# Top-k attention with a token and channel mixer: six of nine probability tiles masked on GpSimd before the exponential and transposed by DMA

## The chip, the cores and the metric

The kernel runs on one core of a Trainium2 chip, in one launch. The metric is the time of that core on the device, in microseconds (us), lower is better; the time of a kernel is the median of its runs. One further execution was recorded by the hardware profiler; its span runs from the core's first to its last instruction.

In the text, PE is TensorE's matmul stream, PEld its weight loads, DVE is VectorE, ACT is ScalarE, POOL is GpSimd and SP is SyncE, whose queue issues the DMAs here. L385 is line 385 of the kernel.

## The reference, cut to what matters

```python
# q, k, v: (8, 8, 576, 64); top_k = 32
scores = (1 / np.sqrt(64)) * np.matmul(q, k.transpose(0, 1, 3, 2))
kth    = np.partition(scores, -32, axis=-1)[..., -32:-31]    # 32nd largest of each row
scores = np.where(scores >= kth, scores, -1e9)
attn   = np.exp(scores - scores.max(-1, keepdims=True))
attn   = attn / (attn.sum(-1, keepdims=True) + 1e-9)
x      = np.matmul(attn, v)               # heads side by side: (8, 576, 512)
h      = np.maximum(x^T @ w_tok1, 0) @ w_tok2 ;  u  = x + h^T      # 576 -> 256 -> 576
h2     = np.maximum(u @ w_ch1, 0) @ w_ch2     ;  out = u + h2      # 512 -> 1536 -> 512
```

Each row of 576 scores keeps its 32 largest; the rest must count as nothing after the exponential.

## The kernel before, in words

**Units and tiles.** The work is 32 units (`NU`), each one batch and one pair of heads. A unit has nine score tiles of 128 rows by 576 columns: tiles 0 to 7 are query block `t = i // 2` of head `i % 2`, tile 8 holds the last 64 rows of both heads. Tiles 0 to 3 form group 0, tiles 4 to 8 group 1. After every fourth unit a batch is whole and its channel mixer runs (`h2_mm`, `out_mm`), spread between the units that follow.

**One group, in order.** PE forms the scores in PSUM (`s0_mm`, `s1_mm`, `st_mm`); ACT copies them into `SS` (four buffers, one per group) or `St` (tile 8). DVE then finds the 32nd largest value of each row. `upper` (L350) takes the larger of each pair of scores 288 columns apart into `hi`; `split4` (L374, twice) pairs `hi` once more into `hh` (larger) and `hl` (smaller). `top_round` takes the eight largest of `hh` per tile (L385) and strikes them out (L388), four rounds. `low_round` takes the eight largest of `hl` and of `lo` (L398), and `combine` (L406, L413, L415, L419) merges the lists into a column of `kthall`, the threshold. `lo`, the smaller of each first pair, is made on POOL from the bits: `both_bits` (L356) adds the two scores' bit patterns and `lower_bits` (L365) subtracts that of the larger. Both L350, L374, L406 and L415 on DVE and L356, L365 on POOL read two tensors from SBUF.

**Masking and transposing.** `expo` (ACT, L456) writes `E`, the exponential of all 576 scores, less the row's maximum (`nmax`, POOL, L447). A mask `U` is above zero where a score lies below the threshold: on ACT in one step for tiles 1, 3, 5, 7, 8 (`below_act`, L492), on POOL in two for tiles 0, 2, 4, 6 (`below` into `z`, L469, then `clamp`, L477), and on DVE in the last group (`below_dve`, L485). PE transposes by matmul against the identity (`both_tr`, L498 for `E`, L501 for `U` against the identity times -2^100) and sums both in PSUM, so that masked places sink far below zero. ACT copies out through a Relu into `PT` (`p_ev`, L521, L525; the last 64 columns of up to four tiles together, `ptail_ev`, L541, L549). `o_mm` (L562) multiplies `PT` by the values, with a column of ones that gives the row sums; DVE inverts the sums (`o_den`, L574, L575) and ACT scales into `Xb` (`o_ev`, L585).

**What sets the order.** The instructions' order on each engine is laid down ahead of time by `Plan`: each step is a task with an engine, a cost, a priority (`U = 100 * u` for unit `u`, plus an offset), its predecessors and the buffers that it takes and gives back; `order` plays this forward and emits the tasks as they would start. On the chip each engine works through its list in that order and waits on semaphores. `hold` and `later` keep POOL's masks of one group behind `lower_bits` of the next. Loads and stores stand on SP's queue (`load_one` L229, `out_st` L698). The weights' casts on POOL (L742) fall into the first units.

At the end an exact second pass runs if a check on `low8` and `kthall` (L1045 to L1055) finds a row whose lists of eight were too short.

Of the kernel before, what the change touches and what calls it, by code (L numbers as in the profile page):

```python
# [12 lines left out]
RSLACK = 3.0  # L13
ACTMASK = (1, 3, 5, 7, 8)
PE_RATE = 0.85
# [90 lines left out]
def kernel(  # L106
# [54 lines left out]
    stp = pool("stp", 2)  # L161
    gp = pool("gp", 2)
    eep = pool("eep", 9)
    uup = pool("uup", 8)
# [39 lines left out]
    for t in lbufs:  # L204
        nc.gpsimd.memset(t[:, :, :, 0:1], BIG)
    kthall = const.tile([P, NU * NTILE], f32, tag="kthall")
    low8 = const.tile([P, NU * NTILE, 2], f32, tag="low8")
# [3 lines left out]
    }  # L211
    ctr = {"vb": 0, "lb": 0}

# [123 lines left out]
    def srow(st, i):  # L337
        return st["St"][:, :] if i == 2 * NT else st["SS", i // 4][:, i % 4, :]

    def halves(st, g):  # L340
        SS = st["SS", g]
        yield slice(0, 4), SS[:, :, 0:HALF], SS[:, :, HALF:S]
        if g:
            St = st["St"]
            yield 4, St[:, 0:HALF], St[:, HALF:S]
# [7 lines left out]
    def both_bits(st, g):  # L353
        x = lists["lo"]
        for at, left, right in halves(st, g):
            nc.gpsimd.tensor_tensor(  # L356
                out=x[:, at, :].bitcast(i32), in0=left.bitcast(i32), in1=right.bitcast(i32),
                op=ALU.add,
            )
        st["lo"] = x  # L360
# [92 lines left out]
    def expo(st, i):  # L453
        g, a = grp(i)
        E = eep.tile([P, S], bf16, name="E", tag="E")
        nc.scalar.activation(  # L456
            out=E[:, :], in_=srow(st, i), func=AF.Exp,
            bias=st["nmax", g][:, a : a + 1], scale=scale,
        )
        st["E", i] = E  # L460

# [4 lines left out]

    def below(st, i):
        z = gp.tile([P, S], bf16, name="z", tag="z")
        nc.gpsimd.tensor_scalar(  # L469
            out=z[:, :], in0=srow(st, i), scalar1=-1.0, scalar2=kcol(st, i),  # L470
            op0=ALU.mult, op1=ALU.add,
        )
        st["z", i] = z

    def clamp(st, i):
        U = uup.tile([P, S], bf16, name="U", tag="U")
        nc.gpsimd.tensor_scalar(  # L477
            out=U[:, :], in0=st.pop(("z", i))[:, :], scalar1=BIG, scalar2=0.0,
            op0=ALU.min, op1=ALU.max,
        )  # L480
        st["U", i] = U

    def below_dve(st, i):
# [53 lines left out]
    def ptail_ev(st, tiles):  # L537
        PT, tl = pt_tile(st), st.pop(("tpl", tiles[0]))
        if len(tiles) > 1:
            t0 = tiles[0] // 2  # L540
            nc.scalar.activation(  # L541
                out=PT[0:TAIL, :, NT, t0 * P : (t0 + 2) * P].rearrange(
                    "p h (t q) -> p t h q", t=2
                ),
                in_=tl[0:TAIL, :].rearrange("p (t h q) -> p t h q", t=2, h=2),
                func=AF.Relu,
            )
        else:
            nc.scalar.activation(  # L549
                out=PT[0:TAIL, :, NT, W:S],  # L550
                in_=tl[0:TAIL, 0:P].rearrange("p (h q) -> p h q", h=2),
                func=AF.Relu,
            )
# [141 lines left out]
    def out_st(mst, sc, b):  # L695
# [10 lines left out]
            ldq=2, ldk=2, ldv=2, vb=NVB, qkT=2, SS=4, St=2, tp=2, s0=3, O=1, mps=2,  # L706
            E=9, U=8, z=2, A=3, lb=2, nmax=3, PT=2, Xb=2, H1T=2, UT=2, H2T=1, ob=2, den=4,
        )
# [65 lines left out]
    later = []  # L774
    masks = []
    chain = {}
# [3 lines left out]
    def plan_unit(u):  # L780
# [22 lines left out]
        )  # L803
        kd, selE, keep = {}, {}, {}
        smm = []
        nms = {}
        for g in range(2):
# [32 lines left out]
            x = add("DVE", 0.30 * n + 0.15, U + 5 * g, lambda g=g: split4(st, g), deps=[x, chain.get("low")])  # L840
            nm = None
            for r in range(TOPK // 8):
                x = add("DVE", (0.21 + (0.28 if r < 3 else 0)) * n, U + 5 * g,
                        lambda g=g, r=r: top_round(st, g, r), deps=[x],
                        acq=[("A", u, g), ("nmax", u, g)] if r == 0 else [])
                if r == 0:
                    nm = add("POOL", 0.25, U - 1000, lambda g=g: neg_max(st, g), deps=[x])
                    lob = add("POOL", 0.65 * n + 0.1, U - 1000, lambda g=g: both_bits(st, g), deps=[nm, chain.get("low")])
                    lob = add("POOL", 0.65 * n, U - 1000, lambda g=g: lower_bits(st, g), deps=[lob])
                    nms[g] = chain["bits"] = lob  # L850
                    for t in later:
                        pl.after(t, lob)
                    later.clear()
                    if g == 0:
                        pl.after(vc, lob)
            x = add("DVE", 0.21 * n, U + 5 * g, lambda g=g: low_round(st, g, 1), deps=[x], acq=[("lb", u, g)])
            x = add("DVE", 0.36 * n, U + 5 * g, lambda g=g: low_round(st, g, 0), deps=[x, lob])
            chain["low"] = x
            x = add("DVE", 0.19 * n + 0.2, U + 5 * g, lambda g=g: combine(st, g, u), deps=[x])
            keep[g] = add("POOL", 0.5, U + 5, lambda g=g: keep_low8(st, g, u), deps=[x], rel=[("lb", u, g)])  # L860
            exps = []
            for i in gtiles(g):
                exps.append(
                    add("ACT", 0.66, U - 50 + i, lambda i=i: expo(st, i), deps=[nm] + exps[-1:] + evs, acq=[("E", u, i)])
                )
            kd[g] = x
            selE[g] = exps
        PTd = {}
        pte = []
        hold = {0: [], 1: later}  # L870

        def evict(dur, prio, fn, tr, key):
            e = add("ACT", dur, prio, fn, deps=[tr] + pte[:1],
                    acq=[] if pte else [("PT", u)], rel=[key])
            pte.append(e)
            return e

        tails = []
        for g in range(2):
            ms, mains = [], []  # L880
            allms = list(masks)
            masks.clear()
            if not (last and g == 1):
                hold[g].append(keep[g])
            order = sorted(gtiles(g), key=lambda i: (i not in ACTMASK, i))
            for at, i in enumerate(order):
                a, w = i - 4 * g, U + 4 * g + at
                if last and g == 1:
                    m = add("DVE", 0.45, w + 20, lambda i=i: below_dve(st, i), deps=[kd[g]] + allms[-4:], acq=[("U", u, i)])
                elif i in ACTMASK:  # L890
                    m = add("ACT", 0.66, w - 20, lambda i=i: below_act(st, i), deps=[kd[g]] + allms[-5:], acq=[("U", u, i)])
                else:
                    x = add("POOL", 0.75, w, lambda i=i: below(st, i), deps=[kd[g]] + ms[-1:], acq=[("z", u, i)])
                    m = add("POOL", 0.68, w - 0.5, lambda i=i: clamp(st, i), deps=[x], acq=[("U", u, i)], rel=[("z", u, i)])
                    hold[g].append(x)
                ms.append(m)
                masks.append(m)
                tr = add("PE", 0.58, w, lambda i=i: p_tr(st, i), deps=[m, selE[g][a]], acq=[("tp", u, i)])
                mains.append(tr)
                PTd[i] = (evict(0.52, w + 20, lambda i=i: p_ev(st, i), tr, ("tp", u, i)))  # L900
            add("POOL", 0.0, U - 1000, lambda: None, deps=ms + selE[g],
                rel=[("SS", u, g), ("A", u, g), ("nmax", u, g)] + ([("St", u)] if g else []))
            for part, tiles in enumerate([list(range(4 * g, 4 * g + 4))] + ([[2 * NT]] if g else [])):
                tr = add("PE", 0.15 * len(tiles), U + 4 * g + 5, lambda tiles=tiles: ptail_tr(st, tiles),
                         deps=mains + selE[g], acq=[("tp", u, "l", tiles[0])],
                         rel=[(r, u, i) for r in "EU" for i in tiles])
                tails.append(
                    evict(0.5 if len(tiles) > 1 else 0.17, U + 30, lambda tiles=tiles: ptail_ev(st, tiles), tr,
                          ("tp", u, "l", tiles[0]))
                )  # L910
        for t in hold[0]:
            pl.after(t, nms[1])
# [142 lines left out]
    with tc.If(flag != 0):  # L1055
        with tc.For_i(0, B, 1) as bv:
            mst = {}
            for p in range(NPAIR):
                st = {}
                for name, src in (("q", q), ("k", k), ("v", v)):  # L1060
# [7 lines left out]
                for g in range(2):  # L1068
# [13 lines left out]
                    for i in gtiles(g):  # L1082
                        expo(st, i)
                        below(st, i)
                        clamp(st, i)
                        p_tr(st, i)
                        p_ev(st, i)
# [52 lines left out]
```

## Time and profile before

| | us |
|---|---|
| three runs: median, lowest, highest | 1067.17, 1065.01, 1068.78 |
| profiled execution, its own time | 1066.77 |
| its span | 1065.0 |
| first DVE instruction of the selection (L350) starts | 15.85 |
| DVE's last threshold (L419) ends | 995.8 |

The page of the profile gives each engine's busy time, share of the span and number of instructions; then 40 slices of the span with a digit for the busy share; then the chain of work that ended last; then groups of instructions with their busy time, the mean of one in ns, and the idle time of the engine just before them with the instruction that ended it. Busy time counts overlapped instructions once, so a group's busy time can be less than its count times its mean. From the trace come three more views: waits (engine and line, what was waited for, sum, times, longest), the timeline (start, duration, engine, line), and windows (busy time of each engine in a stretch with the granted TensorE clock).

| group | count | mean ns |
|---|---|---|
| L385 DVE MAX8, 144 columns | 1152 | 291 |
| L350 DVE TENSOR_TENSOR, 1152 columns | 64 | 1522 |
| L356 and L365 POOL TENSOR_TENSOR, 1152 columns | 96 | 2632, 2630 |
| L469, L477 POOL TENSOR_SCALAR, 576 columns | 126 each | 810, 685 |
| L456, L492 ACT ACTIVATE, 576 columns | 288, 157 | 779, 790 |
| L521 ACT ACTIVATE, 512 columns | 256 | 607 |
| L498 and L501 PE MATMUL, 128 columns, into tpp | 1152 each | 232 |

### The profile page before, as it was taken

The page shows a single profiled execution, that of the slowest core. Times are in us where ns is not written, and L with a number is a line of the kernel's source. Part 1 is how long each engine was busy: PE and PEld are TensorE (multiplying, and loading weights), DVE is VectorE, ACT ScalarE, POOL GpSimd, SP SyncE. Part 2 cuts the span into 40 slices and gives each one's busy share as a digit, 9 for nine tenths or more (in the row PEclk, how much of TensorE's full clock was granted, in tenths as well). Part 3 has the DMA queues.
Part 4 walks back from the last instruction along what each step waited for, and adds up shares of the span by engine and source line. Part 5 has one row for each costly group of instructions (what it writes and reads, how often), then busy time and mean ns, then how long its engine had stood idle before and what let it go on. Part 6 is the DMA issues. An engine that isn't in the chain of part 4 may idle for free.

```text
span 1065.0 us, 23797 instructions
## 1 busy us (share of the span) xinstructions
PE 958.3 (90%) x8058; PEld 572.4 (54%) x8058; DVE 955.8 (90%) x4087; ACT 868.2 (82%) x2008; POOL 635.8 (60%) x626
## 2 busy tenths in 40 slices
PE   7778878999898999999999998999999999899895
PEld 4444545546455556555555565556555555555542
DVE  4999999998999999999999989999799979999501
ACT  5667787988989979988989799898789789898522
POOL 3686667665766576657666666667367647666300
PEclk9676798999989998999989999899989989899878
DMA  7423111012201121112120113002211021000001
GB/s 176 154 73 93 34 35 34 2 32 60 57 12 35 33 59 24 34 45 64 40 57 13 52 29 79 13 20 67 48 25 35 31 50 35 12 2 31 16 2 48
DMA packets 123572, 46.86 MB, mean 44 GB/s; under 512 B 115952, under 2 KB 116528, under 8 KB 123440
## 3 DMA queue, kind: packets, MB, share of 16 engines
q1 hardware_dynamic: 123440, 45.24, 16.4%
q8 instruction: 65, 1.06, 0.4%
q14 instruction: 67, 0.55, 0.2%
HBM read 35.78 MB, written 9.44 MB: 42 GB/s over the span
## 4 chain that ended last, share of the span: by engine, by line
DVE 39%; PE 39%; ACT 17%; issue 1%; DMA 1%; POOL 1%; SPq 0%; DVEq 0%; ACTq 0%; POOLq 0%
DVE A L385 10%; DVE hh L388 10%; PE ps L680 7%; PE s L300 7%; DVE lb L398 6%; PE O L562 5%; PE ps L650 5%; DVE hi L350 5%; ACT E L456 5%; PE tpp L498 3%; PE tpp L501 2%; DVE hh L374 2%; ACT U L492 2%; DVE hl L374 2%; ACT SS L310 2%; ACT PT L521 2%
## 5 line engine op out<-in xcount | busy, mean ns | idle before, releaser
L385 DVE MAX8 A<-hh 128x8 f32<-128x144 f32 x1152 | 263.6, 291 | 0.0
L388 DVE MATCH_REPLACE8 hh<-A,hh 128x144 f32<-128x144 f32 x864 | 241.9, 289 | 0.0
L447 POOL TENSOR_SCALAR nmax<-A 128x4 f32<-128x4 f32 x64 | 15.1, 235 | 328.5 <-DVE A L385 310.4
L300 PE MATMUL s<-qkT 64*128 64x512 f32 x512 | 185.2, 723 | 9.4 <-ACT SS L290 8.0
L498 PEld LDWEIGHTS <-E 128*128 128x128 bf16 (+1 forms) x1440 | 149.0, 106 | 82.2 <-issue 68.0
L365 POOL TENSOR_TENSOR lo<-lo,hi 128x1152 int32<-128x1152 int32 x64 | 188.0, 2938 | 5.0
L456 ACT ACTIVATE E<-SS,nmax 128x576 bf16<-128x576 f32 x256 | 185.1, 779 | 2.1 <-PE tpl L501 1.6
L521 ACT ACTIVATE PT<-tpp 128x512 bf16<-128x512 f32 x256 | 150.0, 607 | 39.9 <-PE tpp L501 38.6
L498 PE MATMUL tpp<-identB,E 128*128 128x128 bf16 x1152 | 169.9, 232 | 11.2 <-ACT PT L521 7.9
L501 PE MATMUL tpp<-identN,U 128*128 128x128 bf16 x1152 | 168.9, 232 | 10.1 <-POOL U L477 9.3
L501 PEld LDWEIGHTS <-U 128*128 128x128 bf16 (+1 forms) x1440 | 153.9, 107 | 36.3 <-issue 18.0
L356 POOL TENSOR_TENSOR lo<-SS 128x1152 int32<-128x1152 int32 x64 | 168.5, 2632 | 0.0
L310 ACT COPY SS<-s 128x512 f32<-128x512 f32 x256 | 141.6, 598 | 32.6 <-PE s L300 31.8
L562 PE MATMUL O<-vb,PT 128*128 128x65 bf16 (+3 forms) x1600 | 125.5, 202 | 12.7 <-ACT Xb L585 12.6
L650 PE MATMUL ps<-UT,wc1b 128*128 128x512 bf16 (+1 forms) x768 | 122.4, 297 | 9.8 <-ACT H2T L663 6.0
L350 DVE TENSOR_TENSOR hi<-SS 128x1152 f32<-128x1152 f32 x64 | 97.4, 1522 | 36.4 <-ACT SS L310 36.4
L562 PEld LDWEIGHTS <-PT 128*128 128x128 bf16 (+3 forms) x1600 | 93.7, 101 | 50.3 <-issue 15.2
L398 DVE MAX8 lb<-lo 128x8 f32<-128x288 f32 x288 | 108.5, 437 | 0.0
L469 POOL TENSOR_SCALAR z<-SS,kthall 128x576 bf16<-128x576 f32 x126 | 102.0, 810 | 6.2
L492 ACT ACTIVATE U<-SS,kthall 128x576 bf16<-128x576 f32 x126 | 96.4, 790 | 8.2 <-DVE kthall L419 8.2
L663 ACT ACTIVATE H2T<-ps 128x512 bf16<-128x512 f32 (+1 forms) x180 | 73.7, 434 | 34.6 <-PE ps L650 34.1
L477 POOL TENSOR_SCALAR U<-z 128x576 bf16<-128x576 bf16 x126 | 86.2, 685 | 18.8 <-PE tpl L501 8.8
(90 smaller groups left out, 1611.8 us busy)
## 6 DMA issues: line engine op xcount, KB each, us to landing
qL<-in_q_dram SPq DMA_DIRECT2D x64, 128.0 KB, 2.4
kL<-in_k_dram SPq DMA_DIRECT2D x64, 128.0 KB, 2.5
vL<-in_v_dram SPq DMA_DIRECT2D x64, 128.0 KB, 2.5
out_dram<-ob SPq DMA_DIRECT2D x32, 256.0 KB, 2.0
wst<-in_moe_w_ch_dram SPq DMA_DIRECT2D x4, 1536.0 KB, 6.7
qL<-in_q_dram SPq DMA_DIRECT2D x32, 32.0 KB, 2.3
kL<-in_k_dram SPq DMA_DIRECT2D x32, 32.0 KB, 2.4
vL<-in_v_dram SPq DMA_DIRECT2D x32, 32.0 KB, 2.3
```

The source lines that it names most:

```text
L300: nc.tensor.matmul(out=x[:, :], lhsT=T[rows[hh], 0, t * P : (t + 1) * P], rhs=T[rows[hh], 1, 0:W], start=True, stop=True,)
L356: nc.gpsimd.tensor_tensor(out=x[:, at, :].bitcast(i32), in0=left.bitcast(i32), in1=right.bitcast(i32), op=ALU.add,)
L365: nc.gpsimd.tensor_tensor(out=x, in0=x, in1=st["hi"][:, 0:n, :].bitcast(i32), op=ALU.subtract)
L385: nc.vector.max(A[:, i, 8 * r : 8 * r + 8], hh[:, i, :])
L388: nc.vector.match_replace(hh[:, i, :], A[:, i, 8 * r : 8 * r + 8], hh[:, i, :], NEG)
L398: nc.vector.max(st["L", g][:, i, j, 1:NLO], x[:, i, :])
L456: nc.scalar.activation(out=E[:, :], in_=srow(st, i), func=AF.Exp, bias=st["nmax", g][:, a : a + 1], scale=scale,)
L498: nc.tensor.matmul(out=out, lhsT=st["E", i][:, cols], rhs=identB[:, :], start=True, stop=False)
L501: nc.tensor.matmul(out=out, lhsT=st["U", i][:, cols], rhs=identN[:, :], start=False, stop=True)
L521: nc.scalar.activation(out=PT[:, hh, 0:NT, t * P : (t + 1) * P], in_=src, func=AF.Relu)
L562: nc.tensor.matmul(out=O[0:ms, t, :], lhsT=PT[0:kz, hh, j, t * P : t * P + ms], rhs=st["vb"][0:kz, j, hh, :], start=(j == 0), stop=(j == N ...
L650: nc.tensor.matmul(out=ps[:, 0 : hi - lo], lhsT=wc1b[:, cc, fc * P : (fc + 1) * P], rhs=mst["UT"][:, cc, lo:hi], start=(cc == 0), stop=(cc ...
```

## The change: what it does

Tiles 0 to 5 of every unit (0 to 3 of the last) are now *turned*. For each group POOL multiplies the thresholds by 2^90 (`raise_kth`); ACT makes a steep mask `U = relu(2^90 * (threshold - score))` (`steep`); POOL subtracts `U` from the scores in place (`sink`, a TENSOR_TENSOR over 128x576, fp32 less bf16); ACT takes the exponential of the sunk scores into one of five buffers `pb` (`expo`), whose columns 576 to 640 are zero; SP issues a DMA that transposes the 128x640 buffer into `PT` (`turn`). These tiles have no matmul transposes and no copies out of PSUM. Tiles 6, 7 and 8 go the former way, their mask always on ACT. `below` and `clamp` are gone.

`both_bits` no longer stands behind the first top round: it follows `split4`, held there by a copy of one column of `hl` into `lo`. `raise_kth` stands behind `both_bits` of the next group, the sinks behind `lower_bits` of the next group, as the POOL masks did. `E` has five buffers instead of nine.

```diff
-ACTMASK = (1, 3, 5, 7, 8)
+STEEP = 2.0**90
+TURNED = (0, 1, 2, 3, 4, 5)
...
+    NP = 5
+    pbufs = [const.tile([P, NS * P], bf16, name=f"pb{i}", tag=f"pb{i}") for i in range(NP)]
+    for t in pbufs:
+        nc.gpsimd.memset(t[:, S : NS * P], 0.0)
...
     def both_bits(st, g):
         x = lists["lo"]
+        nc.gpsimd.tensor_copy(out=x[:, 0, 0:1], in_=st["hl"][:, 0, 0:1])
...
+    def raise_kth(st, g):
+        x = m8p.tile([P, NS], f32, name="kbig", tag="kbig")
+        c, n = st["kth", g], 4 + g
+        nc.gpsimd.tensor_scalar_mul(x[:, 0:n], kthall[:, c : c + n], STEEP)
+        st["kbig", g] = x
+
+    def steep(st, i):
+        g, a = grp(i)
         U = uup.tile([P, S], bf16, name="U", tag="U")
+        nc.scalar.activation(
+            out=U[:, :], in_=srow(st, i), func=AF.Relu,
+            bias=st["kbig", g][:, a : a + 1], scale=-STEEP,
         )
         st["U", i] = U
+
+    def sink(st, i):
+        x = srow(st, i)
+        nc.gpsimd.tensor_tensor(out=x, in0=x, in1=st["U", i][:, :], op=ALU.subtract)
+
+    def turn(st, i):
+        PT = pt_tile(st)
+        t, hh = divmod(i, 2)
+        nc.sync.dma_start_transpose(PT[:, hh, :, t * P : (t + 1) * P], st["P", i][:, :])
...
+            lob = add("POOL", 0.65 * n + 0.3, U - 1000, lambda g=g: both_bits(st, g), deps=[x])
+            sums[g] = lob
+            for t in raised:
+                pl.after(t, lob)
+            raised.clear()
+            lob = add("POOL", 0.73 * n, U - 1000, lambda g=g: lower_bits(st, g), deps=[lob])
+            nms[g] = chain["bits"] = lob
+            for t in later:
+                pl.after(t, lob)
...
-                    lob = add("POOL", 0.65 * n + 0.1, U - 1000, lambda g=g: both_bits(st, g), deps=[nm, chain.get("low")])
-                    lob = add("POOL", 0.65 * n, U - 1000, lambda g=g: lower_bits(st, g), deps=[lob])
...
+                    m = add("ACT", 0.66, U - 20 + i, lambda i=i: steep(st, i), deps=[kb, chain.get("steep")], acq=[("U", u, i)])
+                    chain["steep"] = m
+                    x = add("POOL", 1.32, U + i, lambda i=i: sink(st, i), deps=[m, chain.get("sink")], rel=[("U", u, i)])
+                    chain["sink"] = x
+                    hold[g].append(x)
+                    y = add("ACT", 0.66, U - 15 + i, lambda i=i: expo(st, i), deps=[x, nmx[g], chain.get("pexp")], acq=[("P", u, i)])
+                    chain["pexp"] = y
+                    done.append(y)
+                    deps, acq = to_pt(y)
+                    y = add("SP", 0.7, U - 300, lambda i=i: turn(st, i), deps=deps, acq=acq)
+                    pte.append(y)
+                    PTd[i] = add("DQ", 0.6, U, lambda: None, deps=[y], rel=[("P", u, i)], slack=1.5)
+                    continue
...
-                    x = add("POOL", 0.75, w, lambda i=i: below(st, i), deps=[kd[g]] + ms[-1:], acq=[("z", u, i)])
-                    m = add("POOL", 0.68, w - 0.5, lambda i=i: clamp(st, i), deps=[x], acq=[("U", u, i)], rel=[("z", u, i)])
-                    hold[g].append(x)
```

In the order that results, POOL does this for group 0: the one-column copy, `both_bits`, `raise_kth` of the group before and `nmax`, `lower_bits`, the cast of the values, a sink, the copy into `low8`, a sink. For group 1: the copy, `both_bits` (two instructions), `nmax` and `raise_kth`, `lower_bits`, and four sinks with the `low8` copy before, between or after them.

## The prediction

> **What bounds the kernel now.** I read the page's first part, the chain of waits, the list of waits, and then the timelines of DVE and POOL over one unit.
>
> ```profile
> PE 958.3 (90%) x8058; PEld 572.4 (54%) x8058; DVE 955.8 (90%) x4087; ACT 868.2 (82%) x2008; POOL 635.8 (60%) x626
> ```
>
> PE and DVE look alike here, so the page does not say which one sets the time. The chain that ended last does, read where it repeats:
>
> ```profile
> 916.79 2.28 DVE lb L398 x8
> ...
> 946.35 2.28 DVE lb L398 x8
> ...
> 975.91 2.28 DVE lb L398 x8
> ```
>
> The same instructions recur every 29.56 us, with DVE alone between them: a unit whose only limit is DVE takes 29.56 us. DVE's thresholds of unit 0 end at 47.5 us, those of unit 31 at 995.8 us: 948.3 us for 31 units, or 30.59 each. Where is the other 1.03?
>
> ```profile
> DVE hi L350 <- ACT SS L310: 36.4, 7, 15.8
> ...
> DVE rden L574 <- PE O L562: 17.4, 5, 8.0
> ```
>
> Of the 36.4 us, 15.85 are the start; 20.6 are six waits in mid-run, all where PE carries a channel mixer besides. Of rden's 17.4 us, 3.3 are in mid-run. Together 24 us. The rest, about 8 us, falls in the first three units, where POOL's weight casts stand in DVE's way:
>
> ```profile
> 44.51 2.74 POOL L742 CAST wc1b<-wst 128x3072 bf16<-128x3072 f32 x1
> ```
>
> ```profile
> 45.06 2.25 DVE L415 TENSOR_TENSOR M<-A,lb 128x40 f32<-128x40 f32 x1
> ```
>
> L415 takes 0.20 us elsewhere. It got going about 0.14 us before the cast's end (47.25). So here a DVE instruction with two SBUF inputs waits for a POOL instruction that is under way, whole; MAX8 and MATCH_REPLACE8, with one, keep their 291 and 289 ns whatever POOL does. That is the fact on which this prediction turns.
>
> **The change, part by part.**
>
> *PE.* 190 tiles (31 units of 6, the last 4) lose their transposes. L498 and L501 into tpp are busy 338.8 us for 288 tiles, 1.18 us each: 224 us go, and some 20 more with the 64-row tails. At 22 us of 30 per unit PE no longer holds up DVE at the mixers. I let 20 of the 24 us go; in what is left something is late after all (ACT's H2T copies, 0.61 us each, stand in the same queue as the score copies).
>
> *ACT.* Goes: 190 copies L521 of 0.59 (busy time by count) = 112 us, one L541 per unit of 0.59 = 19 us, part of the other. Comes: 126 masks of 0.79 that POOL made = 100 us. The exponentials stay, but later. 868 becomes about 835 us, 26 of some 30 per unit: below DVE. `expo` of a turned tile now waits for its sink and for the transpose that last read its buffer; queued behind it are copies of scores, which stand about a unit ahead of DVE (SS has four buffers and a group is released about 18 us after its threshold), so a wait of a few us there reaches nobody. I cost it at nothing; without that cover each us of wait per unit is 31 us.
>
> *POOL.* Goes: L469 and L477, 102 + 86 us. Comes: 190 sinks, 64 `raise_kth` and 64 one-column copies of about 0.2 us (nmax takes 0.23). A sink on this shape is in no row. Nearest: the two-input L356 takes 0.795 us for 288 columns and 2.63 for 1152, so 1.40 for 576 by a straight line. The one-input z of the same 576 columns takes 0.75 and is the floor; 2.63 is the ceiling. One operand is bf16, and U with a bf16 input runs 0.08 below z. I take **1.35**, between 1.32 and 1.40. POOL then has about 730 us, not the bound; what counts is where it meets DVE.
>
> *Where POOL meets DVE.* The rows, DVE first, then POOL:
>
> ```profile
> 507.82 0.75 DVE L374 TENSOR_TENSOR hl<-hi 128x576 f32<-128x576 f32 x1
> ...
> 517.59 0.40 DVE L406 TENSOR_TENSOR M<-A,lb 128x256 f32<-128x256 f32 x1
> ...
> 518.81 1.76 DVE L350 TENSOR_TENSOR hi<-SS 128x1152 f32<-128x1152 f32 x1
> ...
> 521.80 0.90 DVE L374 TENSOR_TENSOR hl<-hi 128x720 f32<-128x720 f32 x1
> ...
> 533.96 0.46 DVE L406 TENSOR_TENSOR M<-A,lb 128x320 f32<-128x320 f32 x1
> ```
>
> ```profile
> 509.51 0.22 POOL L447 TENSOR_SCALAR nmax<-A 128x4 f32<-128x4 f32 x1 [5.08 <-DVE A L385]
> 509.70 2.63 POOL L356 TENSOR_TENSOR lo<-SS 128x1152 int32<-128x1152 int32 x1
> 512.41 2.63 POOL L365 TENSOR_TENSOR lo<-lo,hi 128x1152 int32<-128x1152 int32 x1
> 514.98 0.62 POOL L239 CAST vb<-vL 128x512 bf16<-128x512 f32 x1
> ...
> 518.69 0.67 POOL L477 TENSOR_SCALAR U<-z 128x576 bf16<-128x576 bf16 x1
> ```
>
> Before, L350 of group 1 met the U of 518.69 and took 1.76 us, not 1.35: 0.41 lost in most units. After, POOL has nothing left there, and this is won. But the sinks run up to `combine`. I count from the end of `hl`, where the column copy lets POOL start.
>
> Group 0: release 0.08, copy 0.18, release 0.08, `both_bits` 2.63, two small ones 0.42, `lower_bits` with its gap 2.66, values' cast 0.80: 6.85 us. Then a sink, the low8 copy (0.18), a sink: the second runs from 7.03 + s to 7.03 + 2s, that is 8.38 to 9.73. DVE reaches L406 at 517.59 - 508.57 = 9.02 and waits until 0.13 before the sink's end: 9.60. Lost 0.58.
>
> Group 1: 0.34, `both_bits` 3.39 in two parts, small ones 0.40, `lower_bits` 3.25, low8 copy 0.18: 7.56. Four sinks; the third ends at 7.56 + 4.05 = 11.61. DVE reaches L406 at 533.96 - 522.70 = 11.26 and waits to 11.48: 0.22. The fourth sink reads once L406 is done and ends s - 0.13 after it (z of 517.55 ended 0.62 after L406, against 0.75 alone), so it holds DVE for s - 0.26 = 1.09 us; L415 comes 0.55 us after L406's end: 0.54.
>
> Sum 1.34 us per unit, less 0.41: **+0.93**, times 31 = +29 us. By s: 1.32 gives 1.16, 1.40 gives 1.64, below 1.0 nothing.
>
> The Trainium skill, "SBUF — State Buffer", section "SBUF: two separate sides", says the pair of ports is an exclusive lock against any GpSimd instruction that reads SBUF. The 45.06 row agrees; that a two-input POOL instruction holds it as a cast does, only the page says.
>
> *The column hold.* `both_bits` starts 0.75 to 1.0 us sooner after `upper` than before (behind the first L385), and not under L374; the 2.63 us beside one-input DVE work cost nothing. It is in the count above.
>
> *SP and the transposes.* SP issues six more DMAs a unit, 160 KB each; queued behind them are loads (two buffers ahead) and stores. No row shows a transposing DMA. Bounds: a 128 KB load lands after 2.4 us, a 1536 KB one after 6.7. I take 3. Slack: the last sink of a unit ends about 12.5 us into the next, `expo` within 3 us, 3 for the DMA, then O: about 20 us in; DVE's `o_den` stands some 4 us later in its queue. So up to about 6 us nothing waits. The skill's page "VectorE: DVE Perf Modes" ("The three transpose paths") gives 1309 ns for one 128x128 block: five in turn would be an estimated 6.5 us, six tiles 39 us per unit, a time near 1340. Its page "DMA: Bandwidth & Descriptors" ("Latency and other measured facts") gives 261 GB/s, an estimated 0.6 us, and nothing added. No run here shows either yet.
>
> *PE's clock.* Granted: 0.69 in the window 27 to 107 us with PE busy 61 of 80 us, 0.97 in 300 to 480 with 170 of 180. A PE with less to do may get fewer ticks: 22 us per unit (958 - 244, over 32) at the mean 0.92 would be 29.7 at 0.69, still under the unit.
>
> *Ends.* The start is untouched. At the end the last turned tile's PT comes about 3.5 us after DVE's last threshold; O started 3.5 us after it before (999.28). Nothing.
>
> **Sum** on the profiled execution: span 1065 + 29 - 20 = 1074, and 1.8 around it (1066.8 - 1065.0): 1076. The median of the runs shown is 0.4 above the profiled execution, which I neglect.
>
> **Rivals.**
>
> *Faster: the sinks don't meet combine.* If a sink took about 1.0 us, or a two-input POOL instruction didn't hold off DVE, the loss is 0 to 0.4 us per unit: 31 x (0 to 0.4 - 0.41) - 20 to 24 gives 1031 to 1046. For it: no L356 or L365 meets a two-input DVE instruction in the trace, so a two-input hold is not seen. Against: casts, z and U all hold.
>
> *No change.* s = 1.30 and all 24 us regained: L = 1.04, 31 x 0.63 - 24 = -4; with s = 1.32, -1: about 1065.
>
> *Worse: sinks later than counted.* If `steep` stands behind mixer copies in ACT's queue when POOL is ready, the sinks slide past `combine` into L350 and L374 and each meets one more; about 1.0 us per unit, +31: 1107. It decides from ACT being over 3 us late. For it: ACT is 26 us of 30 full. Against: the steep masks need 1.6 us and POOL is busy for 3.3 us more with `lower_bits`.
>
> *Slow transposes.* Over 30.5 / 6 = 5.1 us each on one queue, DMA becomes the bound: at 8 us 190 x 8 = 1520.
>
> **How the numbers follow.** Forecast 0.40, by itself 1069 to 1092 (s from 1.32 to 1.45, waits regained 10 to 24). Faster rival 0.33, no change 0.12, late sinks 0.11, slow transposes 0.04. About 0.3% is what a measurement tells from no change. Faster 0.33, same 0.12, slower 0.55. Range 1036 to 1108: it leaves out slow transposes and the edges of the rivals.
>
> **What would show it.** Right: L406 well above 0.40 and 0.46, L415 above 0.20, L350 of group 1 back at 1.35, L350's waits for ACT nearly gone, a unit near 30.5 us. Wrong: a sink far from 1.35; L406 unmoved; DVE waiting at L350 or L574; a transpose landing after more than 6 us.

## The result and the profile after

| | before | after |
|---|---|---|
| median of 4 runs each on this chip | 1066.49 | 1095.24 |
| lowest, highest | 1065.01, 1068.78 | 1093.59, 1098.16 |
| span of the profiled execution | 1065.0 | 1093.4 |
| thresholds of unit 0 done | 47.5 | 44.9 |
| DVE's last threshold done | 995.8 | 1029.7 |
| from there to the end | 69.2 | 63.7 |
| one unit, mean of units 5 to 31 | 30.48 | 31.48 |

The ratio is 1.0271 [1.0241, 1.03]: slower by 28.8 us, where the forecast said slower by 9. The time lies inside the range, but near its upper end, where the rival "sinks later than counted" stood.

In the changed kernel the lines of the selection moved: L350 is now L354 (`upper`), L374 is L379 (`split4`), L398 is L403, L406 is L411 and L415 is L420 (both `combine`), L419 is L424 (the threshold). On POOL `both_bits` is L361 with its column copy L359, `lower_bits` L370, `raise_kth` L479, the sink L493; on ACT `steep` is L485 and `expo` L466.

From the page of the changed kernel, first the engines' busy time, then the shares of the chain of waits, then two groups (count, busy us, mean ns, idle us before and its releaser; for the DMA the count and the us from issue to landing):

```profile
PE 892.7 (82%) x6083; PEld 491.1 (45%) x6158; DVE 1014.0 (93%) x4087; ACT 838.9 (77%) x1912; POOL 733.7 (67%) x696
...
DVE 92%; PE 5%; issue 1%; DMA 1%; ACT 0%; SPq 0%; DVEq 0%; ACTq 0%
...
L493 POOL TENSOR_TENSOR SS<-SS,U 128x576 f32<-128x576 f32 x190 | 261.0, 1390 | 54.0 <-ACT U L485 53.9
...
PT<-pb SPq DMA_TRANSPOSE x190, 2.4
```

DVE has the same 4087 instructions as before, yet is busy 58 us longer: the instructions themselves became longer. And POOL's sinks stand idle for 54 us waiting for `U`, which ACT makes. The first fact was predicted, at half its size (29 us); the second stood in the prediction only as a rival, and it is what the forecast left out. The list of waits of the changed kernel (sum, times, longest) has for DVE's `upper` and for the sinks:

```profile
POOL SS L493 <- ACT U L485: 53.9, 42, 3.5
...
DVE hi L354 <- ACT SS L314: 15.4, 1, 15.4
```

The 24 us of mid-run waits of DVE are gone: of L350's 36.4 only the start is left, and `rden` has none in units 5 to 31. So, in these units, the whole loss is in longer instructions. Here is one unit on DVE, from the timeline of the changed kernel (start, us, engine, line):

```profile
598.26 0.90 DVE L411 TENSOR_TENSOR M<-A,lb 128x256 f32<-128x256 f32 x1
...
599.98 1.35 DVE L354 TENSOR_TENSOR hi<-SS 128x1152 f32<-128x1152 f32 x1
...
614.72 0.47 DVE L411 TENSOR_TENSOR M<-A,lb 128x320 f32<-128x320 f32 x1
...
615.74 0.64 DVE L420 TENSOR_TENSOR M<-A,lb 128x40 f32<-128x40 f32 x1
...
616.52 2.25 DVE L354 TENSOR_TENSOR hi<-SS 128x1152 f32<-128x1152 f32 x1
618.80 1.72 DVE L379 TENSOR_TENSOR hh<-hi 128x576 f32<-128x576 f32 x1
620.45 1.83 DVE L379 TENSOR_TENSOR hl<-hi 128x576 f32<-128x576 f32 x1
```

Undisturbed, these take 0.40, 1.35, 0.47, 0.20, 1.35, 0.75 and 0.75 us. The first, third and fourth are `combine`, where the prediction put the sinks. The last three are the next unit's `upper` and `split4`: 2.95 us lost in this unit, where the prediction had nothing. POOL and ACT in the same stretch show why. First POOL:

```profile
607.53 0.23 POOL L479 TENSOR_SCALAR kbig<-kthall 128x4 f32<-128x4 f32 x1
607.83 3.25 POOL L370 TENSOR_TENSOR lo<-lo,hi 128x1440 int32<-128x1440 int32 x1
611.02 0.20 POOL L432 COPY low<-lb 128x8 f32<-128x8 f32 x1
614.75 6.90 POOL L493 TENSOR_TENSOR SS<-SS,U 128x576 f32<-128x576 f32 x4 [3.54 <-ACT U L485]
```

Then ACT:

```profile
608.66 0.59 ACT L314 COPY SS<-s 128x512 f32<-128x512 f32 x1 [1.88 <-PE s L304]
...
609.26 0.78 ACT L466 ACTIVATE E<-SS,nmax 128x576 bf16<-128x576 f32 x1
609.93 0.60 ACT L680 ACTIVATE H2T<-ps 128x512 bf16<-128x512 f32 x1
...
612.30 1.12 ACT L602 ACTIVATE Xb<-O,rden 128x64 bf16<-128x64 f32 x5
613.29 0.72 ACT L680 ACTIVATE H2T<-ps 128x512 bf16<-128x512 f32 x2
613.87 0.80 ACT L485 ACTIVATE U<-SS,kbig 128x576 bf16<-128x576 f32 x1
```

The thresholds of this group were ready on DVE at 600.07 (L424). `raise_kth` gave them to ACT only at 607.76, since it stands behind `both_bits` on POOL. ACT made the first mask at 613.87, 6.1 us later: score copies that waited for PE, exponentials, mixer copies and `Xb` stand ahead of it. POOL was free at 611.2 and waited until 614.75. So four sinks that were counted to begin at 611.2 ran from 614.75 to 621.65, through L420, L354 and both L379.

**The accounting.** For units 5 to 31 I summed, over DVE's two-input instructions, what each took beyond its undisturbed time. Per unit:

| us per unit | predicted change | before | after |
|---|---|---|---|
| L411 and L420 (`combine`) | +1.34 | 0.02 | 1.14 |
| L354 and L379 (`upper`, `split4`) | -0.41 | 0.39 | 1.15 |
| DVE idle | -0.65 (-20 us in 31 units) | 0.89 | 0 |

Together 2.29 against 1.30: the 1.0 us by which the unit grew. `combine` came out close to the prediction. The next unit's `upper` and `split4` were to become clean and cost 1.15 instead. Of the selection's instructions only these TENSOR_TENSOR became longer: no MAX8 or MATCH_REPLACE8 over 144 columns takes more than 0.31 us in either kernel. The rest of the span adds up so: 27 units grew by 1.0 us each, the four before them by 9.5 us together, unit 0's thresholds came 2.6 us sooner and the end is 5.5 us shorter, 28.4 us in all.

### The profile page after: what moved, and what is told of

Its sections match the earlier page's. It is cut to its first block, busy times and chain, and to the rows that moved or that the text cites. A ratio compares the mean times of both kernels' runs of the same rounds, so it can differ in the third digit from the quotient of the medians.

```text
span 1093.4 us, 20372 instructions
## 1 busy us (share of the span) xinstructions
PE 892.7 (82%) x6083; PEld 491.1 (45%) x6158; DVE 1014.0 (93%) x4087; ACT 838.9 (77%) x1912; POOL 733.7 (67%) x696
## 4 chain that ended last, share of the span: by engine, by line
DVE 92%; PE 5%; issue 1%; DMA 1%; ACT 0%; SPq 0%; DVEq 0%; ACTq 0%
DVE A L390 22%; DVE hh L393 22%; DVE lb L403 15%; DVE hi L354 10%; DVE hh L379 6%; DVE hl L379 5%; DVE M L411 4%; DVE M L420 3%; DVE A L418 3%; PE ps L667 1%; PE acc L1026 1%; DVE kthall L424 1%; DVE rden L591 1%; DMA out_dram<-ob 0%; PE s L304 0%
## 5 line engine op out<-in xcount | busy, mean ns | idle before, releaser
L493 POOL TENSOR_TENSOR SS<-SS,U 128x576 f32<-128x576 f32 x190 | 261.0, 1390 | 54.0 <-ACT U L485 53.9
L304 PE MATMUL s<-qkT 64*128 64x512 f32 x512 | 209.6, 787 | 28.9 <-ACT SS L294 26.9
L370 POOL TENSOR_TENSOR lo<-lo,hi 128x1152 int32<-128x1152 int32 x64 | 187.9, 2937 | 2.7
L361 POOL TENSOR_TENSOR lo<-SS 128x1152 int32<-128x1152 int32 x64 | 168.0, 2626 | 5.2 <-POOL lo L359 0.2
L359 POOL COPY lo<-hl 128x1 f32<-128x1 f32 x64 | 12.0, 187 | 219.8 <-DVE hl L379 202.0
L485 ACT ACTIVATE U<-SS,kbig 128x576 bf16<-128x576 f32 x190 | 138.7, 781 | 12.4 <-POOL kbig L479 12.3
L466 ACT ACTIVATE pb<-SS,nmax 128x576 bf16<-128x576 f32 x190 | 144.5, 793 | 3.3 <-POOL SS L493 3.3
L667 PE MATMUL ps<-UT,wc1b 128*128 128x64 bf16 (+1 forms) x739 | 123.6, 302 | 27.8 <-ACT H2T L680 23.2
L354 DVE TENSOR_TENSOR hi<-SS 128x1152 f32<-128x1152 f32 x64 | 103.8, 1622 | 15.4 <-ACT SS L314 15.4
L403 DVE MAX8 lb<-lo 128x8 f32<-128x288 f32 x288 | 108.5, 436 | 0.0
L667 PEld LDWEIGHTS <-wc1b 128*128 128x128 bf16 x768 | 55.5, 102 | 102.5 <-issue 68.3
L697 PE MATMUL ps<-wc2b,H2T 128*128 128x512 bf16 (+1 forms) x415 | 96.6, 381 | 0.3
L304 PEld LDWEIGHTS s<-qkT 64*128 64x128 f32 x512 | 62.4, 226 | 73.0 <-ACT SS L294 40.5
L602 ACT ACTIVATE Xb<-O,rden 128x64 bf16<-128x64 f32 (+1 forms) x320 | 70.8, 320 | 29.4 <-DVE rden L592 29.4
L518 PE MATMUL tpp<-identN,U 128*128 128x128 bf16 x392 | 70.6, 265 | 19.4 <-ACT U L509 15.6
L515 PE MATMUL tpp<-identB,E 128*128 128x128 bf16 x392 | 71.6, 264 | 8.6 <-ACT PT L538 3.5
```

The costliest lines, as they stand in the source:

```text
L304: nc.tensor.matmul(out=x[:, :], lhsT=T[rows[hh], 0, t * P : (t + 1) * P], rhs=T[rows[hh], 1, 0:W], start=True, stop=True,)
L354: nc.vector.tensor_tensor(out=x[:, at, :], in0=left, in1=right, op=ALU.max)
L361: nc.gpsimd.tensor_tensor(out=x[:, at, :].bitcast(i32), in0=left.bitcast(i32), in1=right.bitcast(i32), op=ALU.add,)
L370: nc.gpsimd.tensor_tensor(out=x, in0=x, in1=st["hi"][:, 0:n, :].bitcast(i32), op=ALU.subtract)
L403: nc.vector.max(st["L", g][:, i, j, 1:NLO], x[:, i, :])
L466: nc.scalar.activation(out=x, in_=srow(st, i), func=AF.Exp, bias=st["nmax", g][:, a : a + 1], scale=scale,)
```

## The experiments

All are edits of the changed kernel, except that of experiment 5, which edits the kernel before. The theory that I took to the chip: all of the loss is sinks that hold DVE's two-input instructions, and half of it is there because the masks come late from ACT. The rivals: the loss is elsewhere (transposes on SP, PE's lower clock, more work on POOL); or it belongs to sinks as such and not to when they run.

**1. The sink made tiny.** It covers one column of each turned tile, so the other columns of those tiles stay unmasked; every wait and DMA stays.

```diff
-        nc.gpsimd.tensor_tensor(out=x, in0=x, in1=st["U", i][:, :], op=ALU.subtract)
+        nc.gpsimd.tensor_tensor(out=x[:, 0:1], in0=x[:, 0:1], in1=st["U", i][:, 0:1], op=ALU.subtract)
```

> This kernel leaves out the masking of the turned tiles: each sink subtracts in one column of 576 instead of all, so that POOL's instruction stays in its place and its waits stay, and only its length goes (190 x about 1.2 us). Theory (the sinks' hold on DVE's two-input instructions is the whole loss): L354, L379, L411 and L420 go back to 1.35, 0.75 to 0.90, 0.40 to 0.46 and 0.20 us, a unit takes about 29.2 us, the time is 1018 to 1030 us. Rival (the loss comes from elsewhere: transposes, later exponentials, PE's lower clock, the column hold): the time stays above 1080 us.

Measured 1035.89 us, ratio 0.9705 [0.9687, 0.9722]. The excess of DVE's two-input instructions falls from 2.29 to 0.01 us per unit. The groups of this kernel, with shapes kept apart (busy us, mean ns, idle):

```profile
L379 DVE TENSOR_TENSOR hh<-hi 128x576 f32<-128x576 f32 x32 | 24.3, 759 | 1.1
...
L411 DVE TENSOR_TENSOR M<-A,lb 128x320 f32<-128x320 f32 x32 | 15.5, 486 | 0.0
...
L420 DVE TENSOR_TENSOR M<-A,lb 128x40 f32<-128x40 f32 x32 | 6.4, 201 | 1.1
```

and the same groups of the changed kernel:

```profile
L379 DVE TENSOR_TENSOR hh<-hi 128x576 f32<-128x576 f32 x32 | 39.2, 1226 | 1.1
...
L411 DVE TENSOR_TENSOR M<-A,lb 128x320 f32<-128x320 f32 x32 | 22.4, 701 | 0.0
...
L420 DVE TENSOR_TENSOR M<-A,lb 128x40 f32<-128x40 f32 x32 | 19.9, 623 | 1.1
```

So the sinks' length is worth 59 us, and the rest of the change, taken together, does not make the kernel slower: with the same PE work and the same 190 transposes, at a clock of 0.861, it is 32 us faster than the kernel before. The time is some 6 us above what I expected; DVE waits 0.3 us per unit for `O`, and a unit takes 29.61 us, not the 29.2 of pure DVE work.

The Trainium skill, "SBUF — State Buffer", section "SBUF: two separate sides", speaks of an exclusive lock on the shared ports. This pair of kernels agrees (2.29 against 0.01 us per unit), and with a two-input POOL instruction, for which the prediction had no row.

**2. Masks and thresholds early.** `raise_kth` no longer stands behind `both_bits`, and `steep` goes ahead of nearly everything in ACT's list.

```diff
-                        if g:
-                            raised.append(kb)
-                        else:
-                            pl.after(kb, sums[1])
-                    m = add("ACT", 0.66, U - 20 + i, lambda i=i: steep(st, i), deps=[kb, chain.get("steep")], acq=[("U", u, i)])
+                    m = add("ACT", 0.66, U - 300 + i, lambda i=i: steep(st, i), deps=[kb, chain.get("steep")], acq=[("U", u, i)])
```

> The same work in another order: raise_kth goes ahead of both_bits of the next group instead of behind it, and steep is put first in ACT's order, so that the masks are there when POOL comes to the sinks. Theory (the sinks of group 0 come late because ACT's steep masks stand behind mixer copies and waits for PE, and slide into L354 and L379 of the next unit): POOL's wait for U, 54 us, goes; L354 and L379 are mostly free; what is left is about 1.0 us per unit at L411 and L420; 1052 to 1068 us. Rival (POOL's work is too long for the group anyway, whatever ACT does): L354 and L379 stay hit, 1082 to 1096 us.

Measured 1051.55 us, ratio 0.9856 [0.9834, 0.9878]: 44 us below the changed kernel with the same instructions. POOL's wait for `U` is gone, L354 and L379 lose nothing, and the excess is 0.89 us per unit, all but 0.01 of it in L411. The time is half a us under the range that I gave. So most of the loss is not sinks as such: it is when they run. What the sinks still cost in this order is the 16 us between this kernel and the one with tiny sinks.

**3. Which of the two edits.** The priority alone, and `raise_kth` alone:

```diff
-                    m = add("ACT", 0.66, U - 20 + i, lambda i=i: steep(st, i), deps=[kb, chain.get("steep")], acq=[("U", u, i)])
+                    m = add("ACT", 0.66, U - 300 + i, lambda i=i: steep(st, i), deps=[kb, chain.get("steep")], acq=[("U", u, i)])
```

> The changed kernel with steep put first in ACT's order, raise_kth left behind both_bits of the next group. Theory (ACT's order makes the masks late): most of the gain of the early-mask kernel, 1058 to 1078 us. Rival (the 3.5 us that raise_kth spends behind both_bits decide): 1080 to 1095 us.

```diff
-                        if g:
-                            raised.append(kb)
-                        else:
-                            pl.after(kb, sums[1])
```

> The changed kernel with raise_kth ahead of both_bits, steep's place in ACT's order left at its priority. With the priority alone 1070 us were measured, with both 1052. Theory (either half brings the masks in time for most units; together all): 1058 to 1078 us, POOL's wait for U well under 54 us. Rival (ACT's priority alone matters): 1088 to 1098 us.

The priority alone gives 1070.23 us, ratio 1.0034 [1.0021, 1.0047]: 25 us regained, excess 1.34, POOL still 18.4 us in wait for `U`. `raise_kth` alone gives 1049.2 us, ratio 0.9832 [0.9815, 0.9848], better than I expected and the shortest time of all the kernels here that mask every tile (the interval of the kernel with both edits overlaps its own): 18 us below the kernel before and 46 below the changed one. Medians over the units, for group 0's four masks, in us:

| | changed | priority only | `raise_kth` early |
|---|---|---|---|
| threshold done to `raise_kth` done | 7.68 | 7.68 | 1.35 |
| `raise_kth` done to the first mask's start | 3.40 | 2.14 | 1.83 |
| threshold done to the last sink's start | 16.85 | 14.70 | 14.28 |

The next unit's L354 begins about 16.5 us after group 0's threshold. A last sink that starts at 14.3 and takes 1.28 is over by then; one that starts at 16.85 is not. The last sink starts later than 16.5 us in 20 of the 32 units of the changed kernel, in 4 with the priority only and in 2 with `raise_kth` early. The timeline of the kernel with `raise_kth` early has, on POOL:

```profile
607.83 1.26 POOL L479 TENSOR_SCALAR kbig<-kthall 128x4 f32<-128x4 f32 x1 [1.27 <-DVE kthall L424]
...
615.10 3.25 POOL L370 TENSOR_TENSOR lo<-lo,hi 128x1440 int32<-128x1440 int32 x1
618.30 5.00 POOL L493 TENSOR_TENSOR SS<-SS,U 128x576 f32<-128x576 f32 x4
```

and on DVE:

```profile
622.39 1.25 DVE L411 TENSOR_TENSOR M<-A,lb 128x320 f32<-128x320 f32 x1
...
624.20 0.20 DVE L420 TENSOR_TENSOR M<-A,lb 128x40 f32<-128x40 f32 x1
...
624.54 1.35 DVE L354 TENSOR_TENSOR hi<-SS 128x1152 f32<-128x1152 f32 x1
```

The sinks follow `lower_bits` without a gap, as the prediction had counted them. In group 1 only one instruction, L411, meets the last of them: 0.8 us per unit.

**4. Fewer turned tiles.** If each sink costs DVE time, four of them should cost less than six.

```diff
-TURNED = (0, 1, 2, 3, 4, 5)
+TURNED = (0, 1, 4, 5)
...
-    eep = pool("eep", 5)
-    uup = pool("uup", 8)
+    eep = pool("eep", 7)
+    uup = pool("uup", 7)
...
-    NP = 5
+    NP = 4
```

> Four turned tiles per unit instead of six (0, 1, 4, 5: two in each group; two more buffers for E, one fewer for U and for the transposed tiles). Theory: with two sinks in the group of five tiles POOL is done about 1 us ahead of L411, only the group of four tiles loses about 0.5 us; 1034 to 1050 us, if ACT, which takes on some 1.5 us per unit, holds. Rival (two copies out of PSUM more make ACT the late one): DVE waits at L354 for ACT, 1060 us or more.

Measured 1091.06 us, ratio 1.0228 [1.0203, 1.0253]: hardly better than six. The excess is 1.48 us per unit, and new waits came up: 0.89 us of DVE idle per unit at L354 for score copies, and 83.2 us in which POOL waited for `U`. My expectation failed. To part the two effects I put the edits of experiment 2 beside four turned tiles, and beside five (tile 3 back on PE; both also with four `pb`):

```diff
-TURNED = (0, 1, 2, 3, 4, 5)
+TURNED = (0, 1, 4, 5)
...
-            E=5, U=8, P=NP, A=3, lb=2, nmax=3, kbig=3, PT=2, Xb=2, H1T=2, UT=2, H2T=1, ob=2, den=4,
+            E=7, U=7, P=NP, A=3, lb=2, nmax=3, kbig=3, PT=2, Xb=2, H1T=2, UT=2, H2T=1, ob=2, den=4,
```

> Four turned tiles (0, 1, 4, 5) as before, but with the early masks. Theory: the loss of the first four-tile kernel was late masks as well (POOL waited 83 us for U) and waits for ACT; the first part goes: 1035 to 1060 us. Rival (ACT's load alone decides): still 1075 to 1092 us.

```diff
-TURNED = (0, 1, 2, 3, 4, 5)
+TURNED = (0, 1, 2, 4, 5)
...
-            E=5, U=8, P=NP, A=3, lb=2, nmax=3, kbig=3, PT=2, Xb=2, H1T=2, UT=2, H2T=1, ob=2, den=4,
+            E=6, U=8, P=NP, A=3, lb=2, nmax=3, kbig=3, PT=2, Xb=2, H1T=2, UT=2, H2T=1, ob=2, den=4,
...
+        elif tiles[0] < 2 * NT:
+            t, hh = divmod(tiles[0], 2)
+            nc.scalar.activation(
+                out=PT[0:TAIL, hh, NT, t * P : (t + 1) * P], in_=tl[0:TAIL, 0:P], func=AF.Relu
+            )
```

> The early masks of the second kernel, and five turned tiles instead of six (0, 1, 2, 4, 5; tile 3 goes through PE, its last 64 columns copied out by themselves; one more buffer for E, one fewer for the transposed tiles). Theory: in the early-mask kernel the fourth sink in the group of five tiles holds L411 up by 0.79 us per unit; with three it is gone, about 29.4 us per unit: 1026 to 1038 us. Rival (ACT, with some 0.8 us per unit more, makes DVE wait at L354): 1045 us or more, with waits for ACT at L354.

Four give 1079.96 us, ratio 1.0107 [1.0073, 1.0141]; five give 1081.27 us, ratio 1.0148 [1.0114, 1.0182]. What I said of the holds came true, the excess is 0.13 and 0.12 us per unit; what I said of the time did not. From the waits of the kernel with four turned tiles:

```profile
DVE hi L354 <- ACT SS L314: 54.7, 15, 15.6
...
DVE rden L591 <- PE O L579: 24.8, 11, 4.9
```

and of the one with five, whose lines past L569 stand five further on:

```profile
DVE hi L354 <- ACT SS L314: 48.0, 10, 15.9
...
DVE rden L596 <- PE O L584: 26.6, 14, 6.9
```

Giving one or two tiles back to PE trades the hold for waits of DVE, with four turned tiles 2.0 and with five 1.7 us of idle time per unit. Undisturbed units of the kernel with five took 29.24 us, which is the pure DVE unit. These two kernels also have other buffer numbers than that of experiment 2. Two runs with all six tiles turned and the edits of experiment 2 test that: four `pb` instead of five, and then all the numbers of the kernel with four turned tiles (seven `E`, seven `U`, four `pb`).

```diff
-    NP = 5
+    NP = 4
```

> The early-mask kernel, still with six turned tiles, with four buffers for the transposed tiles instead of five, as the kernel with five turned tiles had. It asks whether that kernel's waits for ACT came from the buffers or from ACT's work. Theory (ACT's work and the order laid down for it): within 6 us of the early-mask kernel, 1048 to 1058 us. Rival (the buffer): over 1062 us, with DVE's waits at L354 for ACT.

```diff
-    eep = pool("eep", 5)
-    uup = pool("uup", 8)
+    eep = pool("eep", 7)
+    uup = pool("uup", 7)
...
-    NP = 5
+    NP = 4
```

> This is e6_four_early with all six tiles turned again: the buffers of e6 (seven E, seven U, four pb), both edits of e2_early_steep, TURNED back to tiles 0 to 5. It tells apart what made DVE wait for ACT in e6 (1079.96 us, 1.45 us per unit at L354 and 0.57 at L591). If it is the two tiles that go through PE and ACT again (their transposes, their copies out of PSUM, their place in ACT's list), this kernel gives about e2's time: 1048 to 1058 us, under 0.2 us of DVE idle per unit, and L411's 0.8 to 0.9 us of extra length back. If it is the buffers (one U fewer, two E more, or one pb fewer, and the other order that the plan makes of them), it gives 1068 to 1085 with waits at L354 as in e6.

They give 1052.75 us, ratio 0.9866 [0.985, 0.9882], and 1052.23 us, ratio 0.9855 [0.9839, 0.9872]: the time of experiment 2. So for four tiles it is not the buffers: it is the two tiles that go through PE and ACT again, by their work or by the place it takes in the two lists, that make DVE wait. For five tiles, with yet other buffer numbers, only the four `pb` were tested. Whether PE's queue or ACT's comes late first isn't separated by these runs.

**5. The early sums alone.** On the kernel before, `both_bits` goes behind `split4`, held by the column copy; `lower_bits` and what stands behind it come along, and nothing else of the change is made.

```diff
+        nc.gpsimd.tensor_copy(out=x[:, 0, 0:1], in_=st["hl"][:, 0, 0:1])
...
+            lob = add("POOL", 0.65 * n + 0.3, U - 1000, lambda g=g: both_bits(st, g), deps=[x])
+            lob = add("POOL", 0.73 * n, U - 1000, lambda g=g: lower_bits(st, g), deps=[lob])
...
-                    lob = add("POOL", 0.65 * n + 0.1, U - 1000, lambda g=g: both_bits(st, g), deps=[nm, chain.get("low")])
-                    lob = add("POOL", 0.65 * n, U - 1000, lambda g=g: lower_bits(st, g), deps=[lob])
```

> The kernel before with one part of the change alone: both_bits behind split4, held by the column of hl, lower_bits with it; the POOL masks z and U stay. Theory: POOL is done about 0.8 us sooner, U no longer meets L350 (0.35 us per unit), L406 loses little; the waits for PE stay: 1054 to 1063 us. Rival (z and U now meet L406 and L415 instead): 1064 to 1075 us.

Measured 1058.21 us, ratio 0.9926 [0.9898, 0.9954]. The 0.41 us per unit at L350 is won (excess 0.03), but most of it goes to waits at L350, 1.09 us of idle per unit against 0.77: a unit takes 30.38 us instead of 30.48. Of the 9 us between the two profiled spans, 3.7 lie behind the last threshold. This part of the change helps by itself, a little, and the rest of it costs 37 us.

**6. No column hold.** `both_bits` may start as soon as `lo` is free.

```diff
-        nc.gpsimd.tensor_copy(out=x[:, 0, 0:1], in_=st["hl"][:, 0, 0:1])
```

> The changed kernel without the copy of one column of hl, so that both_bits may start as soon as POOL comes to it and the scores are there. Theory: both_bits (2.6 us, two inputs) then starts before L354 and holds up L354 and L379 by 1 to 2 us per group, while the sinks end earlier and free L411 and L420 (about 1.2 us per unit); slower than the changed kernel, 1100 to 1135 us. Rival (the hold only costs POOL its idle time, 220 us in all): faster, 1070 to 1085 us.

Measured 1199.33 us, ratio 1.1226 [1.1206, 1.1247]: the sign of the theory, but 104 us over the changed kernel where I expected 5 to 40. The excess is 5.47 us per unit. Its timeline, POOL:

```profile
606.75 2.76 POOL L492 TENSOR_TENSOR SS<-SS,U 128x576 f32<-128x576 f32 x2 [3.16 <-ACT U L484]
609.47 2.62 POOL L360 TENSOR_TENSOR lo<-SS 128x1152 int32<-128x1152 int32 x1
```

and DVE:

```profile
609.71 3.60 DVE L354 TENSOR_TENSOR hi<-SS 128x1152 f32<-128x1152 f32 x1
```

`both_bits` now starts just ahead of `upper`, and DVE waits for what is left of it: 3.60 us instead of 1.35. In the changed kernel's line numbers (here one lower behind the missing copy) the excess stands at L354 with 1.25 us, at the small L420 of group 0 with 1.86, and the rest at L379 and at L411 and L420 of group 1.

**7. Each transpose issued twice.** If the transposes are hidden, a second one into the same place should cost little.

```diff
-        nc.sync.dma_start_transpose(PT[:, hh, :, t * P : (t + 1) * P], st["P", i][:, :])
+        for _ in range(2):
+            nc.sync.dma_start_transpose(PT[:, hh, :, t * P : (t + 1) * P], st["P", i][:, :])
```

> The changed kernel with each transposing DMA issued twice, the second into the same place behind the first: 380 instead of 190. Theory (a transpose lands in 2.4 us and nothing is late for it): within 5 us of the changed kernel, 1092 to 1102 us, DVE's wait at L591 unchanged. Rival (the transposes hold up O and so the order of everything behind): over 1105 us.

Measured 1250.18 us, ratio 1.1725 [1.1663, 1.1787]; the expectation fell. The waits of this kernel, first of SP's queue, then of PE and DVE (its lines stand one further on):

```profile
SPq L499 <- DMA PT<-pb: 246.0, 190, 3.1
```

```profile
PE O L580 <- DMA PT<-pb: 164.3, 32, 13.0
...
DVE rden L592 <- PE O L580: 128.2, 40, 7.6
```

The second transpose writes where the first does, so it waits on SP for the first to land: 190 waits of 1.3 us. With two issues of 1.2 us a pair holds the queue for some 3.7 us, and six pairs take 22 us of a unit, which takes 36.6 us here. So this run doubled more than I meant and doesn't say what twelve free transposes would cost. It does say how late transposes show: PE waits for `PT`, DVE for `O`. In the changed kernel PE waits for a `PT` DMA at `O` for 4.3 us in all, and DVE's `rden` has no wait behind it in units 5 to 31: there the transposes are hidden.

## Why the prediction was right in sign and three times too small

- **DVE sets the time.** Right: 92% of the chain after, and every us of a unit's growth is found in DVE's instructions.
- **A two-input POOL instruction holds a two-input DVE instruction.** Right; the tiny sink (experiment 1) shows it. This was the weakest link: the faster rival, with 0.33, stood on its failing or on a shorter sink.
- **The sink's length**, taken as 1.35 us: 1.27 to 1.28 where nothing meets it. A little high.
- **`combine`, +1.34 us per unit**: 1.14 measured (0.53, 0.19 and 0.42 against 0.58, 0.22 and 0.54). Right for group 0, the first of the three. That group 1 agrees is partly luck: as counted, with the third sink at L411 and the fourth at L420, it went in only 6 of units 5 to 30; in the others mostly earlier ones of the four sinks, run late, meet these instructions, or none does. In the unit shown L420 waits for the first of the four. With `raise_kth` early, where the sinks follow `lower_bits` without a gap, the fourth sink meets L411 (0.79) and nothing meets L420.
- **Waits regained, 20 of 24 us**: all 24. Right.
- **The step that failed: "After, POOL has nothing left there, and this is won", and the -0.41 us per unit that hung on it.** The "I cost it at nothing" under ACT speaks of `expo`'s wait for its sink, and that held (3.3 us of ACT's idle time in all); the way of the masks themselves through POOL and ACT has no term in the sum at all. L354 and L379 lost 1.15 us, not 0. That is 31 × 1.15 = 36 us over the forecast; less 6 for `combine`, 4 for the waits and 5.5 for the shorter end, it gives 9 + 36 - 16 = 29 against the measured 28.8. It closes this well by luck, since it takes the rate of units 5 to 31 for all. POOL waited for masks 42 times, 1.3 us in the mean and up to 3.5, and the four sinks slid into the next unit's first instructions.
- **Why it failed.** The mechanism was on record as a rival, with its place and its price (about 1.0 us per unit; measured 1.15). It got 0.11 for the reason that "the steep masks need 1.6 us and POOL is busy for 3.3 us more with `lower_bits`". That compares the work of the masks with POOL's cover, and leaves out where the masks stand in line: `raise_kth` behind `both_bits` on POOL (7.7 us after the threshold), then in ACT's list behind score copies that wait for PE, exponentials that wait for `nmax`, and mixer copies. The edit of `raise_kth` alone (experiment 3) moves only the first of these and takes 46 us off. Both positions could be read from the diff and from the list of tasks before the run; the 26 of 30 us by which I had counted ACT full was the hint that I named and didn't follow.
- **POOL and ACT sums** (about 730 and 835 us): 733.7 and 838.9. Right.
- **The transposes** (3 us taken, between 2.4 and 6.7): 2.4, each issue 1.2 us on SP, and hidden. Right. The Trainium skill, "VectorE: DVE Perf Modes", section "The three transpose paths", gives 1309 ns for a 128x128 block, from which an estimate was 6.5 us for five blocks in turn; the measurement decides: 2.4 us, so five blocks don't take five times one.
- **PE's clock**: the granted mean fell from 0.918 to 0.841 as work left PE, and PE stayed under DVE. Right. The work that leaves, 244 us, was wrong: PE's busy time fell by only 65.6 us (958.3 to 892.7). I had subtracted the busy time of groups that overlap: PE's groups of the kernel before add up to 1268 us, of which the transposes have 430. After, they have 179, and all groups 1058. The matmuls that stay also became longer: the 512 score matmuls of L300, now L304, take 787 ns instead of 723, 1.09 times, as 0.918 is to 0.841. It cost nothing here, since 892.7 over 32 units is 27.9 us.
- **The ends**: taken as nothing; from the last threshold to the end it is 5.5 us shorter, and unit 0's thresholds are done 2.6 us sooner. I didn't look for the cause.

Left open: the 9.5 us by which units 1 to 4 grew; what of PE's and ACT's queues makes DVE wait with four or five turned tiles; and whether the last 0.8 us per unit at L411 with `raise_kth` early can be moved away as well.

## What to carry to other kernels

Where an instruction on one engine holds another engine off, its cost is decided by when it runs, and that by the last of its producers in line: follow the operand back through every in-order queue (here threshold, POOL, ACT, POOL) and add what stands ahead of it there, not what it takes itself. A task of 0.2 us, put behind a long one, can be the most costly placement of a change: here 46 us. And before taking work from the engine that holds others off, ask which queue gets it: four turned tiles instead of six removed the holds and brought more waits than they had cost.

## What the runs showed of the hardware that I had not expected

- The hold goes both ways, for a short POOL instruction too. The prediction had one row of this kind, the z of 517.55 behind L406. In the kernel with `raise_kth` early, the POOL instruction at 607.83 handles four columns, 0.23 us elsewhere; it takes 1.26 us, and ends with DVE's L354 (from 607.66, 1.35 us), and so do the others of this shape, 1.26 us in the mean of 32. Two streams of two-input instructions take turns: in the changed kernel L379 takes 1.72 and 1.83 us instead of 0.75, and the four sinks beside them 6.90 us, where four undisturbed ones take 5.00.
- A transposing DMA of a 128x640 bf16 buffer takes SP 1.2 us to issue, where a load or a store takes 0.4 to 0.6 us, and lands after 2.4 us, as a 128 KB load does. Six in a unit are 7.4 us of a 30 us unit on SP; issued twice, with a wait between (experiment 7), six pairs take 22 us.
